# Attention and MoE on one core: idle matmuls ahead of batch 0's k^T v, k and v tails on both partition halves, and an uneven split of the last chunk

## The chip, the core and the metric

The kernel runs on one core of a Trainium2 chip. The time is the device time of that core in microseconds (us) for one execution, and the median over several executions is compared. TensorE is called PE below, VectorE DVE, ScalarE ACT, GpSimd POOL and SyncE SP, as in the profile.

## The reference

Attention without a softmax over the keys, then a two-layer feed-forward on its output. Shapes: q, k and v have 8 batches, 8 heads, 576 positions and 64 columns a head; the feed-forward has 4608 tokens, 512 columns and 2048 hidden columns.

```python
theta = np.pi / 2.0 * pos / S
def phi(x, c, s):
    r = np.maximum(x, 0.0)
    return np.concatenate([r * c, r * s], axis=-1)
q_p = phi(q, cos_w, sin_w)
k_p = phi(k, cos_w, sin_w)
kv = np.einsum('bhsf,bhsd->bhfd', k_p, v)
z = np.sum(k_p, axis=2)
num = np.einsum('bhsf,bhfd->bhsd', q_p, kv)
den = np.einsum('bhsf,bhf->bhs', q_p, z)[..., None] + 1e-06
attn_out = num / den
x = attn_out.transpose(0, 2, 1, 3).reshape(B * S, H * D)
h = x @ w_in
g = h * (1.0 / (1.0 + np.exp(-1.702 * h)))
out = g @ w_out
```

So each head of a batch needs one small matrix, k^T v (128 x 64, as phi doubles the columns), with the sum z as a 65th column, and then every position of q is multiplied by it.

## The kernel before

**Feed-forward.** The 4608 tokens are cut into 9 blocks of 512 (`for i in range(NBLK)`, line 476). A block has 32 slots: 16 of `mm1` (line 281: four matmuls of 128x512 against w_in, then the activation on ACT at line 286 into a tile g) and 16 of `mm2` (line 321: four matmuls of 128x512 against w_out; four slots make one chunk of 128 tokens, which `evac` copies out of PSUM on ACT and stores from POOL's queue). The order is written out by hand: `at(n, f, ...)` hangs a piece of work behind slot n. Block i carries the attention of batch b = i + 1 in this way.

**Attention of a batch.** The 576 positions are four chunks of 128 and a tail of 64. `load_main` and `load_tail` load them from POOL's queue (q, k and v of batch b + 1 in slot 1 of block i). `prep` (line 207) makes phi on DVE, `prep_v` copies v beside a column of ones. `turn_q` transposes phi(q) by a DMA on SP's queue. `unit_kv` makes k^T v: for batches 2 to 7 that is `kv_half` (line 244), for each of 8 heads five matmuls of 128 rows and 65 columns that add up in PSUM, the fifth on the tail. The tail has 64 positions on partitions 0 to 63; the partitions 64 to 127 of `kp` and `vt` that belong to it are set to zero once in block 1 (lines 491 and 492), so that the fifth matmul can take 128 rows. Batches 0 and 1 have k and v in six chunks of 96 positions instead, with no tail. `kvs_half` copies the result out on DVE (line 248). `unit_num` (line 265) multiplies a chunk of q by it, and DVE divides (lines 271 to 273).

**Batch 0.** Its attention runs ahead of the blocks, from line 422 on, and its order is written out too: 12 matmuls on a tile of zeros (`warmup`, line 75), then per quarter of q the preparation, the transposes on PE (`turn_q0`, line 364), and two more idle matmuls, except after the last quarter. Then phi(k) is made by DVE and ACT (lines 205 and 207), and PE makes k^T v (`kv0`, line 373), the products with q (`num0`, line 382), the transposes of x (`turn_x0`, line 409) and the first matmuls of block 0 (`mm1_first`, line 417).

**PSUM.** `mm_tile` gives one bank of a ring of four, `at_tile` two banks, in a ring of two. A taker waits until the readers of the bank's last content are done.

**The end.** The last chunk of the last block is `mm2_last` (line 345): its 512 output columns are made in two halves of 256, each with 16 matmuls, the first copied out by ACT and stored while the second is made, the second copied by DVE (line 350) and stored. Each store is two DMAs, one on SP's queue and one on ACT's.

Of the kernel before, what the change touches and what calls it, by code (L numbers as in the profile page):

```python
# [9 lines left out]
F32 = mybir.dt.float32  # L10
BF16 = mybir.dt.bfloat16
# [10 lines left out]
def kernel(  # L22
# [9 lines left out]
    nc = tc.nc  # L32
    B, H, S, D = q.shape
    d_model = H * D
# [9 lines left out]
    one = ctx.enter_context(tc.tile_pool(name="one", bufs=1))  # L44
    two = ctx.enter_context(tc.tile_pool(name="two", bufs=2))
# [8 lines left out]
    def rows(c):  # L54
        return 128 if c < 4 else 64

    def wide(b, n):
        return b < 2 and n != "q"

    def krows(b, c):  # L60
        return 96 if b < 2 else rows(c)

    warm = const.tile([128, TB], BF16)
    nc.vector.memset(warm, 0.0)

    def mm_tile():
        return ps.tile([128, TB], F32, name="mm", bufs=4)

    def at_tile():
        return ps.tile([128, 2, 512], F32, name="at", bufs=2)  # L70

    def warmup(n):
        wps = at_tile()
        for _ in range(n):
            nc.tensor.matmul(wps[:, 0], warm[:, 0:128], warm, start=True, stop=True)


    state = {b: {} for b in range(B)}
    SRC = {"q": q, "k": k, "v": v}
# [7 lines left out]
                     in_=SRC[n][b, h0:h1, 0:np_ * t, :].rearrange("h (p c) d -> p h (c d)", c=t))  # L87

    def load_tail(b, n, on=nc.gpsimd):
        if on is nc.gpsimd:  # L90
            t = two.tile([64, 512], BF16, name=n + "t")
        else:
            t = one.tile([64, 512], F32, name=f"{n}t{b}")
        state[b][n, 4] = t
        on.dma_start(out=t.rearrange("p (h d) -> p h d", h=H),  # L95
                            in_=SRC[n][b, :, 512:576, :].rearrange("h p d -> p h d"))

    def load_all(b):
        for n in "qkv":
# [4 lines left out]
    w_out_sb = one.tile([128, FC, d_model], BF16)  # L104
# [9 lines left out]
    pos_i = const.tile([128, NC], I32)  # L114
# [4 lines left out]
    for n in range(2):  # L119
        nc.sync.dma_start(out=q0[:, ts(n, 1024)].rearrange("p (h e) -> p h e", h=4),  # L120
                          in_=q[0, 4 * n:4 * n + 4, 0:512, :].rearrange("h (p c) d -> p h (c d)", c=4))
    nc.gpsimd.iota(pos_i[:, 0:4], pattern=[[1, 4]], base=0, channel_multiplier=4)
    nc.gpsimd.iota(pos_i[:, 4:5], pattern=[[1, 1]], base=512, channel_multiplier=1)
    nc.gpsimd.iota(pos6_i, pattern=[[1, 6]], base=0, channel_multiplier=6)
    load_main(0, "k", 0, 4)
    nc.gpsimd.iota(id_i, pattern=[[1, 128]], base=0, channel_multiplier=-1)
# [31 lines left out]
    kp = one.tile([128, 6, H, 2 * D], BF16, name="kp")  # L158
    vt = one.tile([128, 6, H, VW], BF16, name="vt")
# [22 lines left out]
    def part(b, n, c, h0, h1):  # L182
        if wide(b, n):
            return state[b][n][:96, 0:48 * D].rearrange("p (h c d) -> p c h d", c=6, d=D)[:, c, h0:h1]
        if c == 4:
            return state[b][n, 4].rearrange("p (h d) -> p h d", d=D)[:, h0:h1]
        return state[b][n][:, 0:32 * D].rearrange("p (h c d) -> p c h d", c=4, d=D)[:, c, h0:h1]
# [7 lines left out]
    def qn_slot(b, c):  # L195

        return state[b]["qn4"] if b < 2 and c == 4 else state[b]["qn"][:rows(c), c]

    def prep(b, n, c, h0=0, h1=H, on=(nc.vector, nc.vector)):
        r = rows(c) if n == "q" else krows(b, c)  # L200
        for cs, w in enumerate((cos6, sin6) if wide(b, n) else (cosw, sinw)):
            o = qn_slot(b, c) if n == "q" else kp[:r, c]
            oc, i, wc = o[:, h0:h1, cs * D:cs * D + D], part(b, n, c, h0, h1), w[:r, c:c + 1]
            if on[cs] is nc.scalar:
                nc.scalar.activation(oc, i, AF.Relu, scale=wc)  # L205
            else:
                nc.vector.tensor_scalar(oc, i, 0.0, wc, op0=MAX, op1=MUL)  # L207
# [2 lines left out]
        nc.vector.tensor_copy(vt[:96, :, :, 0:D], state[b]["v"][:96, 0:48 * D].rearrange("p (h c d) -> p c h d", c=6, d=D))  # L210

    def prep_v(b, c, h0=0, h1=H):
        nc.vector.tensor_copy(vt[:krows(b, c), c, h0:h1, 0:D], part(b, "v", c, h0, h1))

    def q_slot(b, c):
# [24 lines left out]
    def kv_half(b, n, kv):  # L240
        r, last = (96, 5) if b < 2 else (128, 4)
        for h in range(4 * n, 4 * n + 4):
            for c in range(last + 1):
                nc.tensor.matmul(kv[:, ds(h % 4 * (D + 1), D + 1)], kp[:r, c, h, :], vt[:r, c, h, 0:D + 1],  # L244
                                 start=(c == 0), stop=(c == last))

    def kvs_half(b, n, kv, copy=nc.vector.tensor_copy, w=D + 1):
        copy(state[b]["kvs"][:, n, :, 0:D + 1],  # L248
             kv[:, 0:4 * w].rearrange("p (h e) -> p h e", h=4)[:, :, 0:D + 1])

    def kvs_new(b):
        state[b]["kvs"] = two.tile([128, 2, 4, VW], BF16, name="kvs")

    def unit_kv(b):
        kvs_new(b)
        kv = at_tile()
        for n in range(2):
            kv_half(b, n, kv[:, n])
        for n in range(2):
            kvs_half(b, n, kv[:, n])  # L260

# [15 lines left out]
    gT = {}  # L277
# [11 lines left out]
    def mm1(i, fc):  # L289
        hps = mm_tile()  # L290
        if (i, fc) == (1, 0):

            mm1_part(hps, i, fc, 0, 448)
            mm1_part(hps, i, fc, 448, TB)
        else:
            mm1_part(hps, i, fc)
        gelu(hps, fc)
# [37 lines left out]
    def mm2_last(i, t):  # L335

        yps = mm_tile()
        ysb = ypool.tile([128, d_model], F32, name="ysb")
        hd = d_model // 2
        for n in range(2):  # L340
            cols = ds(n * hd, hd)
            if n == 1:
                yps = mm_tile()
            for fc in range(FC):
                nc.tensor.matmul(yps[:, 0:hd], gT[fc][:, ds(t * 128, 128)], w_out_sb[:, fc, cols],  # L345
                                 start=(fc == 0), stop=(fc == FC - 1))
            if n == 0:
                nc.scalar.copy(ysb[:, cols], yps[:, 0:hd])
            else:
                nc.vector.tensor_copy(ysb[:, cols], yps[:, 0:hd])  # L350
            for m, (p0, cnt, row, step) in enumerate(pieces(i * 4 + t)):
                (nc.sync if m == 0 else nc.scalar).dma_start(out=out[row:row + (cnt - 1) * step + 1:step, cols],
                                                             in_=ysb[p0:p0 + cnt, cols])
# [82 lines left out]
    for n in range(2):  # L436
        for c in range(6):
            prep(0, "k", c, 4 * n, 4 * n + 4, on=(VE, AC if c > 2 else VE))
    kv_lo, kv_hi = mm_tile(), mm_tile()
    kv0(kv_lo, 0, 4)  # L440
    kv0(kv_hi, 4, 6)
# [34 lines left out]
    for i in range(NBLK):  # L476
        work = {n: [] for n in range(32)}
        b = i + 1

        def at(n, f, *a):  # L480
            work[n].append(lambda: f(*a))

        if b < B:
            if i == 0:
                at(13, unit_num, 0, 4)
                at(13, turn_x, 0, 4)
            k0, k1, ks = (11, 24, (25, 26, 27, 28)) if i == 0 else (0, 12, (17, 19, 21, 23, 25))
            at(k0, prep_new, b)
            if i == 1:

                at(2, nc.vector.memset, kp[64:128, 4], 0.0)
                at(2, nc.vector.memset, vt[64:128, 4], 0.0)

                at(0, prep, 1, "q", 4)
                at(0, turn_q, 1, 4)
                at(14, unit_num, 1, 4)
                at(14, turn_x, 1, 4)
            for c in range(4 if i == 0 else NC):
                at(k0, prep, b, "q", c)
                if i == 0:  # L500
                    at(22 + c // 2, turn_q_at, b, c, AC.copy)
                else:
                    at(k0 + c, turn_q, b, c)
            for c in range(6 if b < 2 else NC):
                at(20 if i == 0 else k1 - 4 + c // 2, prep, b, "k", c)
                if b >= 2:
                    at(k1 - 1, prep_v, b, c)
            if b == 1:
                at(k1 - 1, prep_v_wide, b)
            at(k1, unit_kv, b)  # L510
            for c, k in enumerate(ks):
                at(k, unit_num, b, c)
                if i == 0 and c < 4:
                    at(min(k + 2, 31), turn_x_at, b, c)
                else:
                    at(k, turn_x, b, c)
            if 0 < i and b + 1 < B:
                at(1, load_all, b + 1)
        for n in range(32):
            if n < FC:  # L520
                if i > 0 or n > 3:
                    mm1(i, n)
            elif i == 0:
                mm2(i, n % 4, (n - FC) // 4)
            elif i == NBLK - 1 and n >= 28:
                if n == 28:
                    mm2_last(i, 3)
            else:
                mm2(i, (n - FC) // 4, n % 4)
            for f in work[n]:  # L530
                f()
        if i == 0:
            evac(i, 3, nc.vector)
# [30 lines left out]
```

## Time and profile before

| | |
|---|---|
| median of 8 runs | 301.53 us |
| lowest and highest | 298.62 and 303.67 us |
| the profiled execution | 298.62 us |
| its span, first to last instruction | 296.7 us |
| mean granted PE clock | 0.994 |
| PE busy | 285.5 us (96%) |
| ACT, DVE, POOL busy | 126.2, 106.2, 97.5 us |
| DMA, mean | 134 GB/s |

The profile is one execution. "Granted clock" is the share of the full PE clock that the chip's throttle let through. A row of a group gives line, engine, operation, tiles and shapes, count, then the busy time in us and the mean of one in ns, and then the engine's idle time just before, with what ended most of it. Matmuls overlap: each is longer than the distance from one to the next. The chain of waits is followed back from the last instruction, at each step to what released it.

### The profile page before, as it was taken

The page shows a single profiled execution, that of the slowest core. Times are in us where ns is not written, and L with a number is a line of the kernel's source. Part 1 is how long each engine was busy: PE and PEld are TensorE (multiplying, and loading weights), DVE is VectorE, ACT ScalarE, POOL GpSimd, SP SyncE. Part 2 cuts the span into 40 slices and gives each one's busy share as a digit, 9 for nine tenths or more (in the row PEclk, how much of TensorE's full clock was granted, in tenths as well). Part 3 has the DMA queues.
Part 4 walks back from the last instruction along what each step waited for, and adds up shares of the span by engine and source line. Part 5 has one row for each costly group of instructions (what it writes and reads, how often), then busy time and mean ns, then how long its engine had stood idle before and what let it go on. Part 6 is the DMA issues. An engine that isn't in the chain of part 4 may idle for free.

```text
span 296.7 us, 5123 instructions
## 1 busy us (share of the span) xinstructions
PE 285.5 (96%) x1974; PEld 146.8 (49%) x1974; DVE 106.2 (36%) x357; ACT 126.2 (43%) x215; POOL 97.5 (33%) x117
## 2 busy tenths in 40 slices
PE   7778999999999999999999999999999999999994
PEld 3575456545444554455445544554455444444443
DVE  5841454683490158015811482148214200000000
ACT  6836623663126412651165116511651166127411
POOL 8543270540268025801690159004401200120021
PEclk9979999999999999999999999999999999999999
DMA  7999999599999977995799779975902510011033
GB/s 188 192 204 200 203 197 192 156 129 177 157 208 177 176 118 142 185 192 97 135 183 176 118 139 184 173 126 115 194 5 62 120 41 1 35 71 38 0 70 71
DMA packets 87303, 39.65 MB, mean 134 GB/s; under 512 B 57136, under 2 KB 85040, under 8 KB 87280
## 3 DMA queue, kind: packets, MB, share of 16 engines
q0 software_dynamic: 40848, 27.01, 59.6%
q1 hardware_dynamic: 46272, 12.20, 23.2%
q8 instruction: 15, 0.25, 0.3%
q10 hardware_dynamic: 160, 0.13, 0.2%
q14 instruction: 8, 0.07, 0.1%
HBM read 36.70 MB, written 9.44 MB: 156 GB/s over the span
## 4 chain that ended last, share of the span: by engine, by line
PE 88%; DMA 5%; DVE 3%; ACT 2%; issue 1%; DVEq 0%; ACTq 0%
PE mm L281 40%; PE mm L321 37%; DMA qT<-qn 4%; PE at L265 3%; PE at L244 3%; PE mm L417 2%; DMA q<-in_q_dram 1%; DVE qn L207 1%; PE mm L345 1%; PE mm L373 1%; DVE xb L273 1%; ACT qT L226 1%; ACT kp L205 0%; PE mm L364 0%; ACT xT L411 0%
## 5 line engine op out<-in xcount | busy, mean ns | idle before, releaser
L321 PE MATMUL mm<-w_out_sb,g 128*128 128x512 bf16 x560 | 128.6, 379 | 0.0
L281 PE MATMUL mm<-xT,w_in_sb 128*128 128x512 bf16 (+1 forms) x564 | 123.6, 377 | 0.0
L333 POOL DMA_DIRECT2D out_dram<-ysb x54 | 50.7, 943 | 173.8 <-ACT ysb L331 172.4
L286 ACT ACTIVATE g<-mm 128x512 bf16<-128x512 f32 x144 | 85.6, 598 | 45.8 <-PE mm L281 45.4
L281 PEld LDWEIGHTS <-w_in_sb 128*128 128x128 bf16 x564 | 54.4, 98 | 64.0 <-issue 0.2
L321 PEld LDWEIGHTS <-g 128*128 128x128 bf16 x560 | 52.2, 98 | 56.9
L331 ACT COPY ysb<-mm 128x512 f32<-128x512 f32 x34 | 19.9, 586 | 98.0 <-PE mm L321 94.7
L248 DVE CAST kvs<-at 128x260 bf16<-128x260 f32 x14 | 5.4, 426 | 60.3 <-PE at L244 60.3
L273 DVE TENSOR_TENSOR xb<-at,inv 128x512 bf16<-128x512 f32 (+1 forms) x36 | 24.8, 690 | 1.2
L271 DVE TENSOR_SCALAR den<-at 128x8 f32<-128x8 f32 (+1 forms) x36 | 5.9, 165 | 44.2 <-PE at L265 44.2
L350 DVE COPY ysb<-mm 128x256 f32<-128x256 f32 x1 | 0.4, 425 | 59.4 <-PE mm L345 59.4
L265 PEld LDWEIGHTS <-qT 128*128 128x128 bf16 x272 | 12.9, 98 | 8.7 <-DMA qT<-qn 1.0
L207 DVE TENSOR_SCALAR qn<-q,cosw 128x512 bf16<-128x512 bf16 (+1 forms) x36 | 12.7, 356 | 11.4 <-DMA q<-in_q_dram 11.4
L265 PE MATMUL at<-kvs,qT 128*128 128x65 bf16 x272 | 14.2, 194 | 0.5 <-DMA qT<-qn 0.2
L207 DVE TENSOR_SCALAR qn<-q,sinw 128x512 bf16<-128x512 bf16 (+1 forms) x34 | 13.0, 382 | 0.0
L244 PEld LDWEIGHTS <-kp 128*128 128x128 bf16 (+1 forms) x288 | 9.6, 97 | 1.7
L244 PE MATMUL at<-vt,kp 128*128 128x65 bf16 (+1 forms) x288 | 9.8, 193 | 0.0
L86 POOL DMA_DIRECT2D v<-in_v_dram x10 | 8.2, 827 | 3.0 <-DMA w_in_sb<-in_moe_w_in_dram 3.0
L86 POOL DMA_DIRECT2D k<-in_k_dram x9 | 7.7, 860 | 4.0 <-ACT g L286 3.2
L95 POOL DMA_DIRECT2D kt<-in_k_dram x6 | 7.9, 1315 | 2.2 <-DMA k<-in_k_dram 2.2
L207 DVE TENSOR_SCALAR kp<-k,cosw 128x512 bf16<-128x512 bf16 x24 | 8.4, 350 | 0.0
L207 DVE TENSOR_SCALAR kp<-k,sinw 128x512 bf16<-128x512 bf16 x24 | 8.1, 338 | 0.0
(75 smaller groups left out, 139.1 us busy)
## 6 DMA issues: line engine op xcount, KB each, us to landing
out_dram<-ysb POOLq DMA_DIRECT2D x38, 128.0 KB, 2.9
out_dram<-ysb POOLq DMA_DIRECT2D x16, 256.0 KB, 2.8
q<-in_q_dram POOLq DMA_DIRECT2D x7, 512.0 KB, 8.8
k<-in_k_dram POOLq DMA_DIRECT2D x6, 512.0 KB, 10.7
v<-in_v_dram POOLq DMA_DIRECT2D x6, 512.0 KB, 12.3
w_out_sb<-in_moe_w_out_dram POOLq DMA_DIRECT2D x4, 512.0 KB, 18.5
w_in_sb<-in_moe_w_in_dram POOLq DMA_DIRECT2D x3, 512.0 KB, 12.3
q<-in_q_dram SPq DMA_DIRECT2D x2, 512.0 KB, 4.3
```

Of the source, the lines that this page charges most:

```text
L86: on.dma_start(out=state[b][n][:np_, t * D * h0:t * D * h1].rearrange("p (h e) -> p h e", h=h1 - h0), in_=SRC[n][b, h0:h1, 0:np_ * t, :].r ...
L95: on.dma_start(out=t.rearrange("p (h d) -> p h d", h=H), in_=SRC[n][b, :, 512:576, :].rearrange("h p d -> p h d"))
L207: nc.vector.tensor_scalar(oc, i, 0.0, wc, op0=MAX, op1=MUL)
L244: nc.tensor.matmul(kv[:, ds(h % 4 * (D + 1), D + 1)], kp[:r, c, h, :], vt[:r, c, h, 0:D + 1], start=(c == 0), stop=(c == last))
L265: nc.tensor.matmul(nm[:, h // 4, ds(h % 4 * (D + 1), D + 1)], q_slot(b, c)[:, h, :], state[b]["kvs"][:, h // 4, h % 4, 0:D + 1], start=Tru ...
L273: nc.vector.tensor_tensor(state[b]["xb"][:r, c].rearrange("p (n h) d -> p n h d", n=2), nm4[:, :, :, 0:D], inv[:r].unsqueeze(3).to_broadca ...
L281: nc.tensor.matmul(hps[:, c0:c1], w_in_sb[:, kc, ds(fc * 128, 128)], xT[:, kc, ds(i * TB + c0, c1 - c0)], start=(kc == 0), stop=(kc == KC ...
L286: nc.scalar.activation(g, hps, AF.Gelu_apprx_sigmoid)
L321: nc.tensor.matmul(yps, gT[fc][:, ds(t * 128, 128)], w_out_sb[:, fc, :], start=(fc == 0), stop=(fc == FC - 1))
L331: nc.scalar.copy(ysb, cur[t])
L333: nc.gpsimd.dma_start(out=out[row:row + (n - 1) * step + 1:step, :], in_=ysb[p0:p0 + n, :])
L417: nc.tensor.matmul(first[fc][:, c0:c1], w_in_sb[:, kc, ts(fc, 128)], xT[:, kc, c0:c1], start=(kc == 0), stop=(kc == KC - 1))
```

## The change

Three edits. First, eleven matmuls on the tile of zeros are issued on PE after the last transposes of q and ahead of batch 0's k^T v; `warmup` can take a given tile, here one of the four of `mm_tile`. Second, in batches 2 to 7 the tails of k and v are loaded by two DMAs each, heads 0 to 3 onto partitions 0 to 63 and heads 4 to 7 onto 64 to 127, as 256 columns and not 512. The preparation takes 128 rows and four heads, the position table has the tail's positions on both halves, and the zeros are no longer set. The new function `kv_tiled` takes heads h and h + 4 together: four matmuls of 128 rows for each, and then one of 64 rows for each, on the two halves of the rows and into two banks. Third, the last chunk's columns are cut at 384 and not at 256.

```diff
     def krows(b, c):
-        return 96 if b < 2 else rows(c)
+        return 96 if b < 2 else 128
...
-    def warmup(n):
-        wps = at_tile()
+    def warmup(n, wps=None):
+        wps = at_tile()[:, 0] if wps is None else wps
         for _ in range(n):
-            nc.tensor.matmul(wps[:, 0], warm[:, 0:128], warm, start=True, stop=True)
+            nc.tensor.matmul(wps, warm[:, 0:128], warm, start=True, stop=True)
...
     def load_tail(b, n, on=nc.gpsimd):
...
+        t = state[b][n, 4] = two.tile([128, 256], BF16, name=n + "t")
+        for m in range(2):
+            on.dma_start(out=t[64 * m:64 * m + 64].rearrange("p (h d) -> p h d", h=4),
+                         in_=SRC[n][b, 4 * m:4 * m + 4, 512:576, :].rearrange("h p d -> p h d"))
...
-    nc.gpsimd.iota(pos_i[:, 4:5], pattern=[[1, 1]], base=512, channel_multiplier=1)
+    for m in range(2):
+        nc.gpsimd.iota(pos_i[64 * m:64 * m + 64, 4:5], pattern=[[1, 1]], base=512, channel_multiplier=1)
...
+    def kv_tiled(b, kv):
+
+        for h in range(4):
+            o = [kv[:, n, ds(h * (D + 1), D + 1)] for n in range(2)]
+            for n in range(2):
+                for c in range(4):
+                    nc.tensor.matmul(o[n], kp[:, c, h + 4 * n, :], vt[:, c, h + 4 * n, 0:D + 1], start=(c == 0), stop=False)
+            for n in range(2):
+                r = slice(64 * n, 64 * n + 64)
+                nc.tensor.matmul(o[n], kp[r, 4, h, :], vt[r, 4, h, 0:D + 1], start=False, stop=True)
...
         kv = at_tile()
-        for n in range(2):
-            kv_half(b, n, kv[:, n])
+        if b < 2:
+            for n in range(2):
+                kv_half(b, n, kv[:, n])
+        else:
+            kv_tiled(b, kv)
...
-        hd = d_model // 2
         for n in range(2):
-            cols = ds(n * hd, hd)
+            cols = slice(0, 384) if n == 0 else slice(384, 512)
+            w = 384 if n == 0 else 128
...
             prep(0, "k", c, 4 * n, 4 * n + 4, on=(VE, AC if c > 2 else VE))
+    warmup(11, mm_tile())
     kv_lo, kv_hi = mm_tile(), mm_tile()
...
-                at(2, nc.vector.memset, kp[64:128, 4], 0.0)
-                at(2, nc.vector.memset, vt[64:128, 4], 0.0)
```

The rest of the diff passes the four heads of a tail to `prep` and `prep_v` and the width w to the last chunk's matmuls and copies.

More of the change, by code (lines that the diff above doesn't have):

```diff
@@ L89, in load_tail @@
     def load_tail(b, n, on=nc.gpsimd):
[L90 to L96, printed above, removed]
+        if n == "q":
+            t = state[b][n, 4] = two.tile([64, 512], BF16, name=n + "t")
+            on.dma_start(out=t.rearrange("p (h d) -> p h d", h=H),
+                         in_=SRC[n][b, :, 512:576, :].rearrange("h p d -> p h d"))
+            return
+        t = state[b][n, 4] = two.tile([128, 256], BF16, name=n + "t")
+        for m in range(2):
+            on.dma_start(out=t[64 * m:64 * m + 64].rearrange("p (h d) -> p h d", h=4),
+                         in_=SRC[n][b, 4 * m:4 * m + 4, 512:576, :].rearrange("h p d -> p h d"))
     def load_all(b):
@@ L184, in part @@
             return state[b][n][:96, 0:48 * D].rearrange("p (h c d) -> p c h d", c=6, d=D)[:, c, h0:h1]
+        if c == 4 and n != "q":
+            return state[b][n, 4].rearrange("p (h d) -> p h d", d=D)
         if c == 4:
@@ L202, in prep @@
             o = qn_slot(b, c) if n == "q" else kp[:r, c]
+            if n == "k" and c == 4 and b > 1:
+                h1 = 4
             oc, i, wc = o[:, h0:h1, cs * D:cs * D + D], part(b, n, c, h0, h1), w[:r, c:c + 1]
@@ L212, in prep_v @@
     def prep_v(b, c, h0=0, h1=H):
+        if c == 4:
+            h1 = 4
         nc.vector.tensor_copy(vt[:krows(b, c), c, h0:h1, 0:D], part(b, "v", c, h0, h1))
@@ L344, in mm2_last @@
             for fc in range(FC):
-                nc.tensor.matmul(yps[:, 0:hd], gT[fc][:, ds(t * 128, 128)], w_out_sb[:, fc, cols],
+                nc.tensor.matmul(yps[:, 0:w], gT[fc][:, ds(t * 128, 128)], w_out_sb[:, fc, cols],
                                  start=(fc == 0), stop=(fc == FC - 1))
             if n == 0:
-                nc.scalar.copy(ysb[:, cols], yps[:, 0:hd])
+                nc.scalar.copy(ysb[:, cols], yps[:, 0:w])
             else:
-                nc.vector.tensor_copy(ysb[:, cols], yps[:, 0:hd])
+                nc.vector.tensor_copy(ysb[:, cols], yps[:, 0:w])
             for m, (p0, cnt, row, step) in enumerate(pieces(i * 4 + t)):
```

## The prediction, on record before the run

> **What bounds the kernel now.** I read the chain of waits first. It names the engine that sets the end:
>
> ```profile
> PE 88%; DMA 5%; DVE 3%; ACT 2%; issue 1%; DVEq 0%; ACTq 0%
> ```
>
> TensorE (PE) carries 88% of the chain. From 24.3 us to 292.8 us it works almost without a gap, so time added to PE there lengthens the kernel one for one. The head, before 24.3 us, is different: PE waits there. Read at the width over which the granted clock changes (the clock was half from 17.66 to 21.07 us, 3.41 us), the head looks like this; columns are window, its length, busy PE (instructions), granted clock, share of the DMA engines, GB/s:
>
> ```profile
> 7.43:10.84 3.41, 2.32 (x24) 1.00 1.21 179
> 10.84:14.25 3.41, 2.52 (x44) 1.00 1.26 203
> 14.25:17.66 3.41, 1.58 (x28) 1.00 1.25 209
> 17.66:21.07 3.41, 3.40 (x37) 0.50 1.37 196
> ```
>
> After stretches with 2.32 and 2.52 us of work the clock stayed full; after one with 1.58 us it was halved for the next 3.41 us. I then slid the same window over the head to see where else so little work lies together:
>
> ```profile
> 8.20:11.61 3.41, 1.64 (x18) 1.00 1.27 193
> 9.00:12.41 3.41, 1.57 (x19) 1.00 1.30 201
> 9.80:13.21 3.41, 1.57 (x25) 1.00 1.29 202
> 10.60:14.01 3.41, 2.28 (x39) 1.00 1.27 204
> 14.20:17.61 3.41, 1.63 (x30) 1.00 1.25 209
> ```
>
> There are two thin places: one around PE's wait from 9.89 to 11.58 us, ahead of batch 0's k^T v, and one around its wait from 16.2 to 17.67 us. In this execution only the second was punished. The groups of the parts that change (count, busy total, mean or minimum/median/maximum in ns):
>
> ```profile
> L244 PE MATMUL at<-vt,kp x288: 191/193/197, 46.0 to 219.6; 128*128 128x65 bf16 x120, 96*128 96x65 bf16 x24
> L95 POOL DMA_DIRECT2D kt<-in_k_dram x6 | 7.9, 1315 | 2.2 <-DMA k<-in_k_dram 2.2
> L207 DVE TENSOR_SCALAR kp<-kt,cosw 64x512 bf16<-64x512 bf16 x6 | 2.0, 338 | 0.0
> L345 PE MATMUL mm<-w_out_sb,g x32: 272/272/273, 289.1 to 292.5; 128*128 128x256 bf16 x32
> L350 DVE COPY ysb<-mm 128x256 f32<-128x256 f32 x1 | 0.4, 425 | 59.4 <-PE mm L345 59.4
> ```
>
> and one batch of k^T v in the chain (start, length, count):
>
> ```profile
> 98.21 1.21 PE at L244 x40
> ```
>
> 1.21 us for 40 matmuls is 30 ns each, though each takes 193 ns from start to end: they are pipelined, and 163 ns of each is hidden by the next.
>
> **What the Trainium skill says.** "TensorE: Matmul & The Clock Gate", Part 1, says that the array runs at half clock until it has been busy for a window of about 3.4 us that runs freely, not in step with the kernel, and drops back after an idle one. The trace agrees in the width (3.41 us) and the factor (0.50), and shows that a window that is 46% busy (1.58 of 3.41) is enough for the drop. Part 3 of that page says that matmuls in different row tiles start some 4 ns apart. "TensorEngine Tiling (Array Packing)", Key Properties, says that a change of tiling mode "drains the TensorE". No matmul of this trace uses half of the rows, so neither is shown. Part 2 of the first page counts about 128 cycles for a wavefront to leave the array, 53 ns at the full clock that it gives.
>
> **The change, part by part.**
>
> *Idle matmuls (11 of 128x512).* At full clock a 128x512 matmul of the main loop costs 0.216 us (52 in 11.22 us), so they take 11 x 0.216 = 2.37 us. PE is free at about 9.9 us; k^T v can then start at 12.3 us. Before, five of its matmuls went at 11.58, and 31 more from 12.20 (1.92 us, 62 ns each), ending at 14.12 us. After, 36 x 62 ns = 2.23 us from 12.3: the end is 14.5 us, a **delay of 0.4 us**. Queued behind the idle ones are only those matmuls and, through ScalarE's copy into kvs, everything of batch 0. The idle tile takes a turn of the four mm buffers; its turn comes after the first copy of q^T, which ended before 8.7 us, and the later takers get buffers whose readers are as old as before, so no wait there. SP and POOL are not passed.
>
> What it buys: the first thin place is filled (9.9 to 14.5 us without a gap). Window starts from about 8.1 to 10.0 us held at most about 1.7 us of work, so some 1.9/3.41 = 56% of executions should have been halved there. Half clock for 3.41 us loses at most 1.7 us; the visible stage gives the same size (24 matmuls of line 417 at 106 ns and not 56: 1.2 us; 12 of lines 382 and 409: 0.45 us; sum 1.65 us). So 0.56 x 1.65 = 0.9 us on average, less 0.4 us of delay: 0.5 us on average. The profiled execution, halved only in the second place, which the change doesn't touch, would **lose 0.4 us**. It was the fastest of 8 (298.62 us = 296.7 of span and 1.9 around it); the median is 2.9 us above it and the highest 5.1 us, about what one to three halved windows of 1.65 us would add. A median execution therefore has more to win than the mean: I take **-1.2 us**, one window saved less the delay; the ends are +0.8 (no window saved, and the idle ones partly at half clock) and -2.9 (both places saved: 3.3 less 0.4).
>
> *k^T v with tails in row tiles, batches 2 to 7.* A batch has 40 matmuls before and 40 after: 32 full ones and 8 of 64 rows, in 4 pairs. If the two of a pair run side by side, one slot of 30 ns less 4 ns goes per pair: 6 x 4 x 26 ns = **0.6 us saved**. Against it stand two changes of row tiling per pair, 6 x 4 x 2 = 48. Bounds of one: 0 ns (the 96-row matmuls of batch 1 between 128-row ones kept the 30 ns pace, 48 in 1.45 us, but those may not be another tiling) and 163 ns (the whole hidden latency exposed), so 0 to 7.8 us. As an estimate from that page's count I take half of the 53 ns array depth, 27 ns, since a tile of half the rows is half as deep: **+1.3 us**. Net +0.7 us; ends -0.6 and +7.2. All this is on PE's gapless path.
>
> *The rest of the tails.* Each batch issues four tail DMAs for k and v, not two: 12 more on POOL in all at about 0.7 us (six of the issues have a median of 729 ns; one of 4286 lifts the mean to 1315), 1.4 us per batch. Behind them on POOL's queue are output stores; POOL waits 172 us in total for ysb, and four ysb buffers stand between. The bytes are the same. Loads issued at about 92 to 96 us land some 12 us later and are used from 117 us on: 9 us of cover. The transposes of q on SP's queue share the DMA engines; the one that PE waited for (0.2 us at 79.39 us) may be late by a few tenths. VectorE's tail operations shrink from 512 to 256 columns, about 0.07 us each, and two memsets (0.49 and 0.28 us) go; VectorE was done 1.2 us ahead of PE in that block and 8.8 us ahead in the next, so nothing is won. One more iota on POOL, 0.12 us, delays the first k load; VectorE is busy with q up to 9.2 us, before it needs k. Together: **0**, ends -0.1 and +0.5.
>
> *Last chunk.* 32 matmuls of 256 columns take 3.51 us, 110 ns each; 16 of 384 and 16 of 128 stream the same columns: 0. The last copy is 128 columns and not 256: the 512-column copy on VectorE took 690 ns and the 256-column one 425, so some 290 ns are left, 0.13 us saved; the last stores halve. The larger first stores are issued at about 292.4 us, only 0.7 us ahead of the last and not 1.8, and might hold these up. **-0.15 us**, ends -0.3 and +0.4.
>
> *Sum*: for the median -1.2 + 0.7 + 0 - 0.15 = -0.65 us: 301.53 to about 300.9. For an execution like the profiled one +0.4 + 0.7 - 0.15 = +0.95: 299.6.
>
> **Rivals.** *The clock is the larger thing* and the row tiles cost nothing: -2.9 - 0.6 - 0.15 = -3.65 us, 297.9. For it speak the 5 us of spread between equal executions and the two thin places; against it, that the second place lies after the idle matmuls and keeps its gap. *Every change of tiling empties the array*: 48 x 110 to 163 ns = 5.3 to 7.8 us, less 0.6, with the clock's -1.2 and the end's -0.15: 304.9 to 307.4 us, slower. Its place is line 244's successor in blocks 1 to 6, where nothing covers it. It decides from about 105 ns per change (48 x 105 = 5.0 us; less 1.95 that is +3). For it speaks the skill's sentence and the 163 ns that are hidden now; against it, that array depth alone is 53 ns. *The idle matmuls do not do what they are for*: no median execution was halved in the first place; +0.4 + 0.7 - 0.15: 302.5.
>
> **How the numbers follow.** Change within 1% (about what a measurement of this kernel can tell from none) is 298.5 to 304.5 us. The forecast, small switches and one window saved, gets 0.50 (299.3 to 302.5); the large clock gain 0.22 (297.3 to 299); the emptied array 0.20 (304.5 to 309); the useless fill 0.08. Faster by over 1%: most of the second and a little of the first, 0.25. Slower by over 1%: the third and a little of the others, 0.23. Same: 0.52. The range from 297.8 to 305.8 leaves out the lower end of the second case and the upper half of the third.
>
> **What would show it.** One batch of k^T v in the chain: 1.21 us becomes 1.1 (free), about 1.3 (27 ns), over 2 (emptied). In the head: windows from 8 to 14 us more than 80% busy, k^T v ending at about 14.5 us, and the half clock, if any, only after 17.6 us. At the end: a last copy of some 0.29 us. I am wrong if a batch of k^T v grows by more than 0.6 us, if the clock is halved between 10 and 16 us in spite of the fill, or if PE comes to wait in the main loop for loads or transposes.

## The result and the profile after

| | before | changed |
|---|---|---|
| median | 301.3 us (32 runs) | 303.06 us (11 runs) |
| lowest to highest | 298.62 to 303.93 us | 302.44 to 306.39 us |
| ratio to before, 95% interval | | 1.0093 [1.0059, 1.0127] |
| the profiled execution, its span | 298.62, 296.7 us | 303.44, 301.7 us |

The change makes the kernel slower by 0.9%, about 2.8 us, where 0.65 us less was forecast. Some executions fall into a slower state; the ratios in this document leave these out, and so they are not the quotients of the medians shown.

The chain of waits of the changed kernel, one batch of k^T v (start, length, what), says most of it:

```profile
99.62 0.24 PE at L263 x8
99.86 0.14 PE at L266 x2
100.00 0.35 PE at L263 x8
100.34 0.14 PE at L266 x2
100.48 0.35 PE at L263 x8
100.83 0.14 PE at L266 x2
100.96 0.35 PE at L263 x8
101.31 0.14 PE at L266 x2
101.45 2.69 PE mm L305 x12
```

Line 263 is the full matmuls, line 266 the pairs of 64 rows. The first eight full ones take 0.24 us, 30 ns each, as before. A pair takes 0.14 us, and the eight full ones after a pair take 0.35 us: 0.11 us more than the first eight. The twelve matmuls of line 305 after the last pair take 2.69 us; the same twelve took 2.59 us before:

```profile
99.41 2.59 PE mm L281 x12
```

From 99.62 to 101.45 are 1.83 us; with that 0.10 us a batch costs 1.93 us, against 1.21 us: +0.72 us, six times, **+4.3 us**.

The groups of the pairs and of the last copy in the changed kernel (minimum, median and maximum of one in ns; and busy us, mean ns, idle before):

```profile
L266 PE MATMUL at<-vt,kp x48: 200/200/201, 67.5 to 224.6; 64*128 64x65 bf16 x48
```

```profile
L374 DVE COPY ysb<-mm 128x128 f32<-128x128 f32 x1 | 0.3, 292 | 59.4 <-PE mm L369 59.4
```

A single 64-row matmul is not slow (200 ns from start to end, 193 for a full one); it is the passage that costs. The last copy takes 292 ns and not 425, as reckoned.

The waits of PE in the changed kernel (us in total, times, longest):

```profile
PE at L433 <- DVE xb L425: 1.4, 1, 1.4
PE at L289 <- DMA qT<-qn: 1.0, 1, 1.0
PE mm L441 <- ACT xT L435: 0.7, 1, 0.7
```

The wait ahead of k^T v is gone: the idle matmuls fill it. A wait for a transposed q in block 1 has grown from 0.2 to 1.0 us. Against these losses, the main loop (the first long stretch of mm1 behind the head) began at 25.25 us and not at 25.39, and the last copy and what follows it take 0.1 us less: 4.3 + 0.8 - 0.1 - 0.1 = 4.9 of the 5.0 us between the two spans. Each of the two profiles has one stretch of half clock in the head (from 17.7 us before, from 18.8 us now) and none after it. The medians are less far apart than the spans, for the profile of the kernel before is its fastest execution of 32. A median execution therefore got 2 us or more back from somewhere; the head of the kernel is the place to look.

### The profile page after: what moved, and what is told of

Its sections match the earlier page's. It is cut to its first block, busy times and chain, and to the rows that moved or that the text cites. A ratio compares the mean times of both kernels' runs of the same rounds, so it can differ in the third digit from the quotient of the medians.

```text
span 301.7 us, 5168 instructions
## 1 busy us (share of the span) xinstructions
PE 292.2 (97%) x1985; PEld 149.6 (50%) x1985; DVE 104.2 (35%) x355; ACT 126.2 (42%) x215; POOL 101.3 (34%) x130
## 4 chain that ended last, share of the span: by engine, by line
PE 89%; DMA 5%; DVE 3%; ACT 1%; issue 0%; DVEq 0%; ACTq 0%
PE mm L305 39%; PE mm L345 37%; DMA qT<-qn 4%; PE at L289 3%; PE at L263 2%; PE mm L441 2%; DMA q<-in_q_dram 1%; PE mm L369 1%; DVE qn L215 1%; PE at L266 1%; PE mm L397 1%; PE mm L75 1%; DVE xb L297 1%; ACT qT L236 1%; PE at L254 0%; PE mm L388 0%
## 5 line engine op out<-in xcount | busy, mean ns | idle before, releaser
L357 POOL DMA_DIRECT2D out_dram<-ysb x54 | 49.7, 924 | 165.7 <-ACT ysb L355 161.1
L98 POOL DMA_DIRECT2D kt<-in_k_dram x12 | 8.8, 747 | 3.9 <-DMA v<-in_v_dram 2.3
L263 PE MATMUL at<-vt,kp 128*128 128x65 bf16 x192 | 9.9, 194 | 0.0
L98 POOL DMA_DIRECT2D vt<-in_v_dram x12 | 7.7, 654 | 6.7 <-issue 3.1
L215 DVE TENSOR_SCALAR kp<-k,sinw 128x512 bf16<-128x512 bf16 x24 | 9.0, 373 | 0.0
L263 PEld LDWEIGHTS <-kp 128*128 128x128 bf16 x192 | 7.6, 97 | 2.1
```

The source lines that it names most:

```text
L98: on.dma_start(out=t[64 * m:64 * m + 64].rearrange("p (h d) -> p h d", h=4), in_=SRC[n][b, 4 * m:4 * m + 4, 512:576, :].rearrange("h p d - ...
L263: nc.tensor.matmul(o[n], kp[:, c, h + 4 * n, :], vt[:, c, h + 4 * n, 0:D + 1], start=(c == 0), stop=False)
L357: nc.gpsimd.dma_start(out=out[row:row + (n - 1) * step + 1:step, :], in_=ysb[p0:p0 + n, :])
```

## Experiments

All ratios are to the kernel before, run beside them on the same chip; its own median was 300.5 us in the first series, 301.75 in the second and 300.45 in the third.

### The parts alone

*The idle matmuls alone.*

```diff
...
+    warmup(11, mm_tile())
     kv_lo, kv_hi = mm_tile(), mm_tile()
```

> The kernel before with the eleven idle matmuls alone. Theory (the row tiles cost, the idle matmuls win): the changed kernel's trace shows 4.3 us of loss in six batches of k^T v and 0.8 us in a wait for a transpose, but its median rose by 1.8 us only, so the idle matmuls should save some 2 to 3 us in the median: 298.5 to 299.3 us, with less spread. k^T v of batch 0 ends within 0.4 us of the time before. Rival (the idle matmuls do nothing for the clock): 301.3 to 301.7 us, the same spread as before.

Measured: 299.59 us (22 runs), **0.9947 [0.9921, 0.9972]**: 0.8 to 2.4 us saved, 1.6 in the middle, where 2 to 3 were expected (the two medians are 0.9 us apart). k^T v ends at 14.03 us against 14.12. The rival falls, and the granted clock of the executions, below, says the same. The spread didn't shrink (296.95 to 303.34 us).

*The last chunk alone.*

```diff
-            cols = ds(n * hd, hd)
+            cols = slice(0, 384) if n == 0 else slice(384, 512)
...
```

> The kernel before with the last chunk cut at 384 columns alone. All theories: the last copy takes 292 ns and not 425, so -0.13 us, 301.2 us, not to be told from no change. If the larger first stores held the last ones up, +0.2 to +0.5 us, and the time from the last copy to the end of the span would grow above 3.4 us.

Measured: 301.47 us (14 runs), 1.0013 [0.9981, 1.0044]: not to be told from no change.

*The tails alone* (the layout, the four DMAs a batch and `kv_tiled`); in part:

```diff
...
-        for n in range(2):
-            kv_half(b, n, kv[:, n])
+        if b < 2:
+            for n in range(2):
+                kv_half(b, n, kv[:, n])
+        else:
+            kv_tiled(b, kv)
```

> The kernel before with the tails on both halves and the row tiles alone. Theory (each change between full rows and half rows exposes some 104 ns on PE): a batch of k^T v takes 1.93 us with the first matmul after it and not 1.21, six batches +4.3 us; with the wait for the transpose in block 1 up to +5.1: 305.6 to 306.4 us. Rival (the row tiles cost only what the median moved, the idle matmuls do nothing): +1.8 us, 303.1 us. Rival (the four tail DMAs a batch are the loss, through late loads and transposes): the same total, but with waits of PE that add up to more than 3 us.

Measured: 304.03 us (6 runs), **1.0106 [1.0061, 1.015]**: 1.8 to 4.5 us lost. The middle, 3.2 us, is less than the 4.3 of the trace, which lies inside the interval. PE has no wait for q's transposes in this profile, so the third reading falls for the main loop. Its longest wait, 2.6 us for batch 0's v, lies in the head; the last chunk's profile, with loads as before, has one of 1.8 us for the same load. The first rival's +1.8 us lies at the edge of the interval: the median alone does not refute it. The trace does: from the start of the main loop to the end of the span it takes 275.3 us (28.79 to 304.1), the kernel before 271.3 us (25.39 to 296.7), neither with a halved clock in that part. So do the series with 4, 8 and 16 changes below.

*The DMAs alone*: each tail of k and v loaded by two DMAs.

```diff
+        for m in range(1 if n == "q" else 2):
+            h0, h1 = (0, 8) if n == "q" else (4 * m, 4 * m + 4)
+            on.dma_start(out=t[:, h0 * D:h1 * D].rearrange("p (h d) -> p h d", d=D),
+                         in_=SRC[n][b, h0:h1, 512:576, :].rearrange("h p d -> p h d"))
```

> The kernel before with each tail of k and v loaded by two DMAs and nothing else (same bytes, same layout, matmuls of 128 rows). Theory: twelve more issues on POOL are hidden, 301.3 us within 0.3. Rival (they make the transposes of q late): the 0.8 us of wait in block 1 comes here too, 302.1 us or more.

Measured: 301.41 us (22 runs), 1.0021 [0.9993, 1.0048]. Nothing that can be told, although 0.8 us of wait in block 1 does stand in its profile. That wait is not tied to the DMAs: it stands in the fill's profile too, with 2.0 us, and in the last chunk's, with 0.7 us, both without any more DMAs. Nor is it a matter of PE's coming early: in five profiles (before, DMAs alone, last chunk, fill and changed kernel) the first transpose of q is issued 33.5 us after the start of the main loop, so the transposes move along with PE. What differs is how long they take from that issue until the one that PE waits for has landed: 20.4, 21.1, 21.0, 22.2 and 22.0 us, with waits of 0.2, 0.8, 0.7, 2.0 and 1.0 us. Why they take longer in one execution than in another stays open.

### What one change of tiling costs

Batches 2 and 3 have 16 changes each, 4 and 5 have 8, 6 and 7 have 4; and there is one extra matmul on the zeros after each mm1 slot of the last two blocks, whose r, the number of its rows, is 64 in block 7 and 128 in block 8. The idle matmuls and the uneven last chunk are left out.

```diff
-            kv_tiled(b, kv)
+            (kv_16, kv_8, kv_4)[(b - 2) // 2](b, kv)
...
+                    nc.tensor.matmul(pr[:, 0:65], warm[:r, 0:128], warm[:r, 0:65], start=True, stop=True)
```

> The tails kernel with three orders of k^T v: batches 2 and 3 give each head its tail right after its four full matmuls (16 changes of tiling a batch), 4 and 5 the changed kernel's order (8), 6 and 7 put the tails of heads h and h+1 together between the full ones (4). In blocks 7 and 8, which have no attention, one extra matmul of 65 columns on the zeros follows each of the 16 slots of mm1: of 64 rows in block 7, of 128 rows in block 8. Theory (each change exposes about 104 ns, whatever its partner): 2.87, 1.93 and 1.52 us a batch, with the first matmul after it counted in; the mm1 half of block 7 is 32 x 0.104 = 3.3 us longer than that of block 8. Rival (the cost belongs to the pair, through two tiles that write at once): 16 changes with no pair side by side cost no more than 8, about 1.9 us or less. Rival (only the load of the weights is exposed, which a 512-column matmul ahead hides): the batches as in the theory, but block 7 less than 1.7 us longer than block 8.

Measured in one execution (311.17 us), of which only the stages are compared. The chain of waits with 16 changes, in part:

```profile
102.96 0.23 PE at L264 x4
103.19 0.13 PE at L265
```

and with 4:

```profile
196.15 0.24 PE at L283 x8
196.39 0.17 PE at L289 x4
196.56 0.59 PE at L283 x16
197.14 0.17 PE at L289 x4
197.31 0.35 PE at L283 x8
197.66 2.59 PE mm L335 x12
```

With 16 changes four full matmuls and one of 64 rows take 0.36 us, where five slots of 30 ns are 0.15: 0.21 us for two changes. With 4 changes a batch takes 197.66 - 196.15 = 1.51 us; with 8, in the same trace, 134.48 to 136.31 us and 0.10 after it: 1.93 us; with 16, from 70.67 to 73.44 us and 0.10 after it: 2.87 us. Expected were 1.52, 1.93 and 2.87. Against the 1.21 us without a change, that is **about 104 ns for each change** with 16 of them, where no tails stand side by side; with 8 and with 4 it is 100 to 103 ns, when the 0.1 us is added back that such tails save in a batch. A lone 64-row matmul takes 0.13 us and a pair 0.14, so the two of a pair do run side by side, for some 10 ns more than one; the rival that blames the pair falls.

The mm1 halves of blocks 7 (64 rows) and 8 (128 rows), two slots of each, from the chain of waits:

```profile
246.74 0.97 PE mm L335 x4
247.85 0.97 PE mm L335 x4
...
279.00 0.86 PE mm L335 x4
279.90 0.86 PE mm L335 x4
```

A slot with its extra matmul takes 1.10 us in block 7 and 0.895 in block 8; the 16 slots take 17.54 and 14.32 us, and the mm2 half that follows 13.92 us in block 7 and not 13.81, since the last change falls into it. The difference is 3.22 + 0.11 = 3.33 us, 104 ns for each of 32 changes; 3.3 was expected. So 512-column neighbours hide no more of it than 65-column ones, and the third reading falls as it was put. What the trace shows besides is the order of the weight loads, the rows of PEld. In block 8 and in block 7 (start, length, of the loads ahead of the extra matmul):

```profile
278.60 0.10 PEld L578 LDWEIGHTS <-warm 128*128 128x128 bf16 x1
```

```profile
246.54 0.09 PEld L578 LDWEIGHTS <-warm 64*128 64x128 bf16 x1 [0.42 <-issue]
```

The extra matmul itself started at 278.81 us in block 8, 0.21 us after its load, and at 246.54 us in block 7, at the same time as its load. Among full rows the weights are loaded while the matmul ahead runs; across a change of tiling that overlap is gone. The two loads that are laid bare per extra matmul, 93 ns for 64 rows and 98 for the full ones after it, make 191 of the 208 ns by their size. Whether the 104 ns are the load or a wait for the array to empty is still not separated by these runs: both would come at the same place.

### What the idle matmuls save, and where it goes

The granted clock of the last-chunk kernel, whose head is that of the kernel before (window, its length, busy PE, clock, DMA share, GB/s):

```profile
9.70:13.11 3.41, 1.57 (x26) 1.00 1.26 190
13.11:16.52 3.41, 3.41 (x39) 0.50 1.24 206
16.42:19.83 3.41, 1.58 (x29) 0.99 1.32 202
19.83:23.24 3.41, 3.41 (x39) 0.52 1.30 204
```

Here both thin places were punished, each after 3.41 us with less than half of work. The first is the one that the profile of the kernel before only suggested; the profiles of the tails alone and of the kernel with 4 to 16 changes have a halved clock there too. With the idle matmuls no profile has one there; in the changed kernel the same stretch is full:

```profile
10.00:13.41 3.41, 3.41 (x38) 1.00 1.27 200
12.00:15.41 3.41, 3.21 (x59) 1.00 1.24 202
```

The mean granted clock of the other executions says how often. One stretch of 3.41 us at half clock lowers the mean over 297 us by 0.0057: the profile of the kernel before has one such stretch and a mean of 0.994, that of the last chunk two and 0.989. In the second series, where the idle matmuls alone were measured again, their 22 executions have means from 0.991 to 1.000, on average 0.995; the 44 of the kernel before that they are compared with have 0.975 to 0.994, on average 0.985. So the idle matmuls spare an execution between one and two halved stretches.

The time gains less than that. Of the executions with a mean of 0.993 or 0.994, about one halved stretch, the 17 with the idle matmuls took 300.1 us on average and the 6 of the kernel before 298.8: at the same clock 1.3 us more. Something is given back. The fill's first profile shows one place; it halved the clock there:

```profile
73.77:77.18 3.41, 3.41 (x31) 1.00 1.44 176
77.18:80.59 3.41, 1.45 (x14) 1.00 1.55 169
80.59:84.00 3.41, 3.41 (x17) 0.50 0.80 212
```

PE began the main loop at 24.01 us, 1.4 us earlier than in the profile before, since the second thin place was not punished in this execution. At an equal clock the start hardly moves: the profile of the DMAs alone, without idle matmuls and at full clock throughout, has it at 24.22 us, and the changed kernel's, with the second place halved, at 25.25 us against 25.39. In block 1 PE then waited 2.0 us for a transpose of batch 2's q, which landed at 79.7 us (at 79.35 us in the profile before). The wait thinned a stretch, and the clock was halved for the next one; from the start of the main loop to the end of the span are 274.7 us, against 271.3 before. In the profile of the repeat this wait is 0.2 us, so how much of the 1.3 us it makes up is not shown.

I tried to remove that wait by issuing batch 3's loads later.

```diff
-                at(1, load_all, b + 1)
+                at(1 if i > 1 else 10, load_all, b + 1)
```

> The kernel before with batch 3's loads issued in slot 10 of block 1 and not in slot 1, so that they don't run beside the transposes of batch 2's q. Theory (PE's wait in block 1 for a transposed q is made by those loads): the wait, 0.2 us in the profile before and 0.7 to 2.0 in four others, goes; 300.0 to 300.8 us. Rival (the transposes are slow by themselves): the wait stays, 300.5 to 301.3 us.

> The eleven idle matmuls and the late loads. Theory (part of what the idle matmuls win early is given back in block 1, where PE then waits 2 us for a transpose and, in the profile of the fill alone, the clock was halved again after it): more than the sum of the two, 297 to 298.2 us. Rival (no giving back in the median): the fill's 1.6 us and nothing more, 298.9 us.

> The same with six more idle matmuls in PE's wait ahead of the transposes of x, the second thin place. Theory (a stretch of 3.4 us that is about half busy or less halves the clock, wherever it lies): no halved stretch before 25 us in the profile, some 40% x 1.65 us = 0.7 us less than with one fill, 296.5 to 297.5 us, and less spread. Rival (the halving comes from something else, or the six delay the transposes): no less, or up to 0.5 us more, than with one fill.

Measured: 0.9994 [0.9965, 1.0023] for the later loads alone, 0.9952 [0.9925, 0.9979] with the fill, and 0.9954 [0.9929, 0.9979] with two fills. The edit was a miss: between slots 1 and 10 of block 1 nothing else stands on POOL's queue, so the order of instructions on every engine's queue is what it was, and the loads were still issued at 57 to 63 us in the two profiles with fills. The first is thus a second measurement of the kernel before, and the second one of the idle matmuls alone, at 0.9947 and 0.9952. The third has the second fill:

```diff
+    warmup(6, mm_tile())
     turn_x0(nb0, 1, 0, (0, 1))
```

The clock is what was expected: full in every stretch from 8 to 24 us of its profile, and 0.998 on average over its executions against 0.995 with one fill. Yet there is no gain over one fill that can be told, where 0.7 us was expected. The wait for q stands in its profile again:

```profile
PE at L265 <- DMA qT<-qn: 2.0, 1, 2.0
```

As the profile of one fill has it once with 2.0 and once with 0.2 us, that does not show by itself why the second fill gains nothing.

The next pair puts the loads behind the first output stores of block 1, where POOL really has to wait.

```diff
-                at(1, load_all, b + 1)
+                at(1 if i > 1 else 19, load_all, b + 1)
```

> The eleven idle matmuls, and batch 3's loads moved behind the first output stores of block 1 (slot 19), which holds them on POOL's queue until about 75 us; in slot 10 they were issued at 57 to 62 us as before, since nothing stands between on POOL. Theory (those loads make the transposes of batch 2's q late): the last one lands before 74 us and not at 78 to 80, PE's wait in block 1 goes; 298.5 to 299.2 us against 299.6 to 300 with the idle matmuls alone. Rival (the transposes are slow by themselves): they still land at 78 us or later, no gain. What is late next would be batch 3's k in block 2.

> The same with the six more idle matmuls in the second thin place. Theory (with the wait of block 1 gone, what the second fill wins is kept): 0.7 us less than with one fill, 297.5 to 298.5 us, ratio 0.985 to 0.990. Rival (another wait takes it): no less than with one fill.

Measured: 1.0012 [0.9988, 1.0036] and 1.0011 [0.9983, 1.004]; the gain of the idle matmuls is lost. SP's queue shows the first half of the theory right. The transposes of batch 2's q with one fill alone and then with the later loads (start of the first, time to the end of the last issue):

```profile
57.53 15.73 SPq L219 DMA_TRANSPOSE qT<-qn  x5
```

```profile
59.53 7.06 SPq L219 DMA_TRANSPOSE qT<-qn  x5
72.47 12.17 SPq L236 DMA_TRANSPOSE xT<-xb  x6
```

Without the loads beside them they take 7 us and not 16, and the wait for q is gone. But the loads now run beside the next transposes on that queue, those of x, and PE waits for transposes of x at the heads of blocks 2 and 3, 1.7 us in total with one fill and 3.0 with two:

```profile
PE mm L281 <- DMA xT<-xb: 1.7, 2, 1.4
```

The longer of the two, 1.4 us with one fill and 1.9 with two, is the one in block 3. It lies beside the loads of batch 4, whose place was not changed: POOL issued them 3.6 us later than in the fill's profile (q at 96.24 and not at 92.63 us), after waiting 3.0 us for DVE's copies of v. So the delay seems to be handed on. The load of 1.7 MB (three DMAs of 512 KB and three of 64) must lie somewhere, and in both places tried PE came to wait for a transpose.

The kernel with the idle matmuls alone is faster than the kernel before by about half a per cent (0.9947, and 0.9952 in the repeat), and so faster than the changed one; none of the others tried is faster than it by an amount that can be told.

## Why the prediction was wrong

**The step that failed** is this term: "As an estimate from that page's count I take half of the 53 ns array depth, 27 ns, since a tile of half the rows is half as deep: **+1.3 us**." The mechanism was named, the 48 changes were counted rightly, and the bounds 0 and 163 ns held the truth; the value in the middle was wrong. Each change costs 104 ns, so 48 cost 5.0 us, and less the 0.6 us of the pairs 4.4 us; the trace shows 4.3. With that, the prediction's own sum is -1.2 + 4.4 - 0.15 = +3.05 us; +2.8 was measured. The prediction had put the point from which the emptied array decides at "about 105 ns per change". The argument for 27 ns took the wave's passage through half of the rows as the only thing to be waited for. What the trace shows lost is an overlap: the weights' load, 92 to 98 ns, no longer runs beside the matmul ahead. Whether it or the emptying of the array makes up the 104 ns stays open; but the 97 ns of a load stood in the trace before as a row of its own, and as a middle would have come close. The sentence of the Trainium skill that the prediction quotes ("TensorEngine Tiling (Array Packing)", Key Properties), that a change of tiling mode drains the engine, is borne out as a cost at each change; it gives no price.

**The pairs**: expected to save 26 ns each by running side by side; a second tail costs some 10 ns more than one. Right, and small.

**The idle matmuls**: -1.2 us expected in the median, -1.6 [-2.4, -0.8] measured. The mechanism is right: the place of the first thin stretch was punished in the profiles of three kernels without the fill, though not in the one that I had, and in none with it. That the size came out is in part luck, for three terms were off and offset one another: the fill spares between one and two halved stretches and not one, and the delay of 0.4 us did not come: in the changed kernel's profile PE was free at 9.7 us and not at 9.9, and the 36 matmuls took 2.03 us and not 2.23, so that k^T v of batch 0 ended at about the same time as before. The third is what is lost again later, 1.3 us at an equal clock, which the prediction did not have. For the wait at the transposed q in block 1 it allowed a few tenths; profiles of the fill alone have 2.0 and 0.2 us.

**The rest of the tails**: 0 expected; 1.0021 [0.9993, 1.0048] for the DMAs alone, so a loss of more than 1.4 us is excluded and a smaller one is not.

**The last chunk**: -0.15 us expected, +0.4 [-0.6, +1.3] measured: the copy is shorter by 133 ns, and the whole is not to be told from nothing.

**The rivals**: the emptied array was the likely course and had 0.20; I gave the small switch 0.50 because I priced it by one reason only.

## What to carry to other kernels

Before 64-row matmuls are woven into full-row ones, count the passages between the two and not the slots that a pair saves: here a pair saves some 20 ns and costs two passages of 104 ns, so padding the tail with zeros to full rows is the cheaper way. Where an operation has no price in the trace, ask which overlap it breaks and take the price of what is laid bare. A gain on PE in the head can be lost again at a transfer that PE waits for later, so read the waits behind the place of the gain, and in more than one profile: the same wait was 2.0 us in one and 0.2 us in another. Moving the loads away from one transpose made PE wait for others.

## What was not expected of the hardware

A change between 128-row and 64-row matmuls costs about 104 ns on TensorE whether the neighbour has 65 or 512 columns. The clock was halved after stretches of 3.41 us in which PE was busy for 1.45 to 1.76 us (43% to 52%: 1.45 in the main loop of the fill, 1.57 to 1.62 in the heads above, 1.76 in the head with one fill and the loads at slot 19). Such a stretch does not always do it: one with 1.38 us, around a wait of 2.0 us too, was followed by the full clock in the profile with two fills (76.22 to 79.63 us). Five DMA transposes of 128 positions took more than twice as long to issue beside 1.7 MB of loads: 16 us, against 7 us without them.
